# Two expert layers on one core: the out-projection spread over the products, a one-function gate in steps, wider slot tiles, and weights converted in place

## The chip, the cores and the metric

The kernel runs on one core of one Trainium2 chip. The metric is the device time of one execution in microseconds (us). Before the change the median of three runs is 2063.8 us (2063.78 to 2065.51). One further execution was profiled; everything called a row below comes from that one. Engines: PE is TensorE, DVE is VectorE, ACT is ScalarE, POOL is GpSimd, and SP is the queue that starts most transfers.

## What is computed

```python
def _attn_ref(x, state):                    # x (8,8,512,64), state (8,8,32,64)
    scores = x @ state^T / 8 ;  xread = softmax(scores) @ state
    scores2 = state @ x^T / 8 ; sread = softmax(scores2) @ x
    return concat([xread, sread], axis=2)   # 8 x 544 tokens of 512 numbers

def _moe_ref(x, expert_emb, tau, w1, w2):   # 8 experts, 512 -> 1024 -> 512
    idx, gate = the expert with the largest cosine to the token, its probability
    out[t] = gate[t] * (relu(x[t] @ w1[idx]) @ w2[idx])

def _moe2_ref(x, w_gate, w_val, w_out):     # dense, 512 -> 1536 -> 512
    g = x @ w_gate
    return (g * sigmoid(g) * (x @ w_val)) @ w_out
```

The three weights of the dense layer arrive as 64-bit floats. All products are float32 to nearly full precision: an operand is split into a high part H and a low part L, and one product is three matmuls (H by H, H by L, L by H; `mm3`, L136).

## The kernel before, in words

**Order of the work.** Python generators ("streams", L44 to L79) write the instructions of each engine in one fixed order. `main` is the stream that leads; at each of its yields every other stream gets one turn, and a stream that yields n sleeps for n turns. A yield of a function holds a stream back until the function is true; while `main` is held back, only the others put instructions into the queues. These waits exist only while the order is written. On the chip each engine runs its own queue strictly in that order and waits for semaphores, so an instruction that waits holds everything behind it on its engine.

**Stage 1, attention and the routed experts** (`attn_a`, `attn_b`, `route`, `groups` L593). The 8 batches of 512 tokens go mostly to one expert each. `groups` runs 8 batches of 8 pieces (n = 0 to 64); the result of a batch is scaled into the tile `xo` and stored to DRAM as `x2d[u]` (L642, L643).

**Stage 2, conversion** (stream `later`, `convert` L883). The dense weights are cut into 6 column pairs p. For each p six raw tiles (512 KB) are loaded (L901), narrowed from 64 to 32 bits (one ACT square L940, four DVE instructions L876 to L881), and combined by DVE into nine forms k = 0 to 8. `put` (L903) splits a form into the tile `cut` (ACT for H, POOL for L) and POOL starts its store to `w2d` (L907). The stream `homes` (L975) loads the forms of p = 0 to 2 back into their resident places, 2 transfers each (L973). `raw` and `cut` have two buffers each.

**Stage 3, the dense layer** (`moe2` L1035). There are 54 steps (u, p): eight units u of 512 tokens (R = 4 blocks of 128), and unit 8 of 256 tokens (R = 2), each by 6 pairs p. Only three pairs of weights are resident, so the order is units 0 to 6 by p = 0 to 2, unit 7 by p = 0 to 5 (weights replaced behind it: `refill`, L1149), units 0 to 5, then 8, then 6 by p = 3 to 5 (weights of p = 0 to 2 come back behind unit 6), and unit 8 by p = 0 to 2. A unit's first half is stored to `part` and added at its second half.

A step is seven Strassen-like products of 12 matmuls each (`prod`, L1106) into three PSUM banks, with adds between them that read a bank before the next product may go on accumulating in it:

```python
yield from prod(0, 0, True);  a = copy(bank 0)            # ACT,  L1128
yield from prod(1, 1, True);  u2 = bank 1 + a             # DVE,  L1130
yield from prod(0, 2);        Y[:, :, 0, 0] = copy(bank 0)  # ACT, L1132
yield from prod(1, 3);        u4 = bank 1 + a             # DVE,  L1134
yield from out(1)                        # 4 pieces for y1 of the step before
yield from prod(2, 4, True);  yield from prod(1, 5);  gate(1)
yield from out(0)                        # 4 pieces for y0 of the step before
yield from prod(2, 6);        gate(0)
```

`gate(j)` (L1119) is Sigmoid on ACT (L1121), two DVE products (L1122, L1123), and a split into `y{j}H` (ACT) and `y{j}L` (DVE). `out(j)` is the out-projection: R pieces of three matmuls 512 wide into `acc`. When a unit ends with "add", each piece loads its `old` from `part` first (L1056; one buffer) and DVE adds it (L1063). `x_forms` (L988) makes the seven operand forms xf0 to xf6 of the next unit from `x2r`, one after each product of the unit's last step; H is ACT's, L is DVE's.

**Beside it, unit 8's routed experts** (`slots` L759, `slots_scatter` L850), after the conversion: 8 slots, each 32 weight tiles of 128 x 256, loaded by SP (four buffers), split by ACT and DVE, two matmuls each; one PSUM buffer `ps` is shared by products and transposes. `main` can't fetch unit 8 before they are done (L1096).

Of the kernel before, what the change touches and what calls it, by code (L numbers as in the profile page):

```python
# [81 lines left out]
class W:  # L82
# [6 lines left out]
    obs = 2  # L89
    x_lo = ("dve",)  # L90
# [16 lines left out]
    s_gap = (4, 4)  # L107
# [3 lines left out]
    c_gap = (0, 2)  # L111
    c_lo = ("pool",)


class Kernel:
# [30 lines left out]
    def setup(self, cp, kp, dp):  # L146
# [12 lines left out]
        self.tauv = cp.tile([128, 32], F32, name="tauv")[:, 0:1]  # L159
        nc.sync.dma_start(self.tauv, self.tau.to_broadcast([128, 1]))  # L160
# [24 lines left out]

        cp.tile([128, 32], F32, name="fill_c")
# [139 lines left out]
    def attn_b(self, b):  # L326
# [132 lines left out]
    def spread_gate(self, g, R, u):  # L459
# [12 lines left out]
        pp, tag = (self.pa, "pa") if isinstance(u, int) else (self.pq, "pq")  # L472
# [120 lines left out]
    def groups(self):  # L593
# [12 lines left out]
        for n in range(65):  # L606
# [25 lines left out]
            for c in range(4):  # L632
                if prev is not None:
# [4 lines left out]
                    if pf == 7:  # L638
                        xo = self.hp.tile([128, 512], F32, tag="xo", name=f"xo{pb}_{c}", bufs=4)
# [119 lines left out]
    def slots(self):  # L759

        nc, lp = self.nc, self.lp
        regs = {}
        todo = [(e, i, k, c) for e in range(NCHK) for i, k, c in
                [(0, k, c) for k in range(4) for c in range(4)] + [(1, k, c) for c in range(2) for k in range(8)]]
        raw, w, at = {}, {}, [0, 0]

        def load():
# [8 lines left out]
            raw[n] = lp.tile([128, 256], F32, tag="raw", name=f"sraw{n}", bufs=4)  # L776
            nc.sync.dma_start(raw[n], src[ds(regs[e], 1), rows * 128:rows * 128 + 128, cols * 256:cols * 256 + 256]
# [3 lines left out]
        def split():  # L781
            n = at[1]
            if n == len(todo):
                return
            w[n] = [lp.tile([128, 256], F32R, tag="w" + k, name=f"sw{k}{n}", bufs=4) for k in "HL"]
            self.split(*w[n], raw.pop(n), lo_eng=W.s_lo[n % len(W.s_lo)])
            load()
            at[1] += 1

        for _ in range(4):  # L790
            load()
        for _ in range(3):
# [6 lines left out]
        n = 0  # L799
        x = load_x(0)  # L800
        for e in range(NCHK):
            hp = lp.tile([128, 8, 2, 64], F32R, tag="hp", name=f"shp{e}", bufs=1)
            yield W.s_gap[0]
            for k in range(4):
                ps = self.ps.tile([128, 512], F32, tag="ps", name=f"psl{e}_{k}")
                for c in range(4):
                    wH, wL = w.pop(n)
                    nc.tensor.matmul(ps[:, :256], x[:, c, :], wH, start=c == 0, stop=False)  # L808
                    nc.tensor.matmul(ps[:, :256], x[:, c, :], wL, start=False, stop=c == 3)
                    n += 1  # L810
                    split()
                    yield n % 2
                lo = lp.tile([64, 256], F32, tag="lo", name=f"slo{e}_{k}", bufs=1)
                nc.scalar.activation(lo, ps[64:128, :256], AF.Copy)
                hs = lp.tile([64, 256], F32, tag="hs", name=f"shs{e}_{k}", bufs=1)
                nc.vector.tensor_add(hs, ps[0:64, :256], lo)
                yield W.s_gap[1]
                pt = self.ps.tile([128, 512], F32, tag="ps", name=f"pst{e}_{k}")
                for i in range(2):
                    nc.tensor.transpose(pt[:, i * 64:(i + 1) * 64], hs[:, i * 128:(i + 1) * 128],  # L820
                                        self.ident[:64, :64])
                v = pt[:, 0:128].rearrange("p (i k) -> p i k", i=2)
                h = hp[:, 2 * k:2 * k + 2]
                nc.scalar.activation(h[:, :, 0, :], v, AF.Relu)
                nc.vector.scalar_tensor_tensor(h[:, :, 1, :], v, 0.0, h[:, :, 0, :].bitcast(F32),  # L825
                                               op0=ALU.max, op1=ALU.subtract)
            if e < NCHK - 1:
                x = load_x(e + 1)
            yield W.s_gap[1]
            for c in range(2):  # L830
                ps = self.ps.tile([128, 512], F32, tag="ps", name=f"sacc{e}_{c}")
                for k in range(8):
                    wH, wL = w.pop(n)
                    hl = hp[:, k].rearrange("p a k -> p (a k)")
                    nc.tensor.matmul(ps[:, :256], hl, wH, start=k == 0, stop=False)
# [549 lines left out]
```

## Time and profile before

| | |
|---|---|
| median of 3 runs | 2063.8 us |
| the profiled execution: its time, its span | 2068.23 us, 2066.8 us (1.4 us lie around the span) |
| busy share of the span | PE 75%, DVE 55%, ACT 33%, POOL 15% |
| granted clock of PE, mean | 0.862 |
| transfers | 227 MB, 29% of 16 DMA engines from SP's queue, 5% from POOL's |
| stage 1 alone | 0 to about 480 us |
| stage 1 with the conversion | 480 to 610 us |
| dense layer with the conversion | 610 to 850 us |
| dense layer with the slots | 850 to about 1640 us |
| dense layer alone | to 2067 us |

How to read the rows: in a timeline the columns are start, duration, engine, line, operation, output and inputs, count, and in brackets the idle time before and what ended it. Busy PE time overlaps itself (a matmul starts before the one in front has ended), so the pace of PE is read from the starts. A granted clock of 1 is 2.4 GHz, 0.5 is 1.2 GHz.

### The profile page before, as it was taken

The numbers are of one execution on the slowest core, as the hardware profiler recorded it, in microseconds if no ns is written. First come the engines' busy times: TensorE is split into PE (matmuls) and PEld (weight loads), VectorE is DVE, ScalarE is ACT, GpSimd is POOL, SyncE is SP. The second block draws the span as 40 slices with busy tenths as digits, with TensorE's granted clock in tenths as the row PEclk, the third lists the DMA queues.
The fourth block names the chain that finished last, engine by engine and source line by source line (L and its number), as shares of the span: only waits on it lengthen the run. The fifth ranks groups of instructions, "written<-read, shape, count | busy, mean of one in ns | idle before, by whom it ended". The sixth has DMA issues, their size and how long they took to land. (4 is left out here: it accounts for less than half of the span.)

```text
span 2066.8 us, 25792 instructions
## 1 busy us (share of the span) xinstructions
PE 1540.1 (75%) x8941; PEld 1361.6 (66%) x8942; DVE 1139.3 (55%) x2210; ACT 691.8 (33%) x1404; POOL 314.4 (15%) x316
## 2 busy tenths in 40 slices
PE   5799999997554444777878787888776866867876
PEld 4678787775443443676767677777766765756765
DVE  5677667785563665564555564555554533442432
ACT  4445455543322232333333333333332211211211
POOL 2343443332333323000000000000000000000000
PEclk8899999998676776898899999999977988987986
DMA  2243333244757544222223136622223121011441
GB/s 66 88 120 111 90 108 119 67 133 139 276 195 263 205 157 172 81 81 77 57 87 95 39 100 202 197 74 89 78 79 96 59 67 61 6 47 56 163 151 45
DMA packets 172619, 227.25 MB, mean 110 GB/s; under 512 B 49848, under 2 KB 114360, under 8 KB 170304
## 3 DMA queue, kind: packets, MB, share of 16 engines
q1 hardware_dynamic: 158992, 186.98, 28.8%
q0 software_dynamic: 13296, 38.28, 5.1%
q8 instruction: 72, 1.18, 0.2%
q14 instruction: 67, 0.55, 0.1%
q10 hardware_dynamic: 192, 0.26, 0.1%
HBM read 166.74 MB, written 68.16 MB: 114 GB/s over the span
## 5 line engine op out<-in xcount | busy, mean ns | idle before, releaser
L1112 PE MATMUL pq<-xf2H,hm 128*128 128x256 f32 (+1 forms) x432 | 125.9, 367 | 265.7 <-ACT u L1128 265.6
L1112 PEld LDWEIGHTS pq<-xf2H,hm 128*128 128x128 f32 x432 | 98.6, 262 | 275.1 <-ACT u L1128 275.1
L1121 ACT ACTIVATE sg<-Y 128x512 f32<-128x512 f32 (+1 forms) x108 | 65.5, 607 | 346.3 <-DVE Y L1139 177.4
L134 DVE TENSOR_TENSOR swL<-sraw,swH 128x256 fp32r<-128x256 f32 x256 | 104.1, 420 | 76.3 <-ACT swH L130 75.0
L141 PE MATMUL acc<-hH,w1H 128*128 128x512 f32 x256 | 111.6, 436 | 45.1 <-ACT w1H L130 34.0
L1112 PE MATMUL pq<-xf3H,hm 128*128 128x256 f32 (+1 forms) x432 | 119.7, 352 | 28.1 <-DVE u L1130 28.0
L1122 DVE TENSOR_TENSOR sg<-Y,sg 128x512 f32<-128x512 f32 (+1 forms) x108 | 75.0, 694 | 109.1 <-ACT sg L1121 109.1
L130 ACT ACTIVATE swH<-sraw 128x256 fp32r<-128x256 f32 x256 | 100.0, 409 | 84.6 <-PE psl L808 45.6
L1112 PEld LDWEIGHTS pq<-xf3H,hm 128*128 128x128 f32 x432 | 97.8, 259 | 32.5 <-DVE u L1130 32.4
L142 PE MATMUL acc<-hL,w1H 128*128 128x512 f32 x256 | 105.7, 413 | 8.5 <-DVE hL L622 8.5
L143 PE MATMUL acc<-hH,w1L 128*128 128x512 f32 x256 | 106.7, 417 | 3.9 <-POOL w1L L134 3.6
L1112 PE MATMUL pq<-xf1H,hm 128*128 128x256 f32 (+1 forms) x432 | 96.0, 299 | 5.0 <-DVE Y L1139 5.0
L1112 PE MATMUL pq<-xf5H,hm 128*128 128x256 f32 (+1 forms) x432 | 90.7, 288 | 5.7 <-DVE u L1134 5.7
L1112 PE MATMUL pq<-xf0H,hm 128*128 128x256 f32 (+1 forms) x432 | 93.5, 294 | 0.0
L1112 PE MATMUL pq<-xf6H,hm 128*128 128x256 f32 (+1 forms) x432 | 90.5, 289 | 3.9 <-DVE Y L1137 3.8
L141 PEld LDWEIGHTS acc<-hH,w1H 128*128 128x128 f32 x256 | 51.2, 200 | 58.0 <-ACT w1H L130 38.4
L1112 PE MATMUL pq<-xf4H,hm 128*128 128x256 f32 (+1 forms) x432 | 88.3, 284 | 0.0
L141 PE MATMUL o<-hm,y1H 128*128 128x512 f32 x204 | 86.1, 422 | 0.0
L808 PE MATMUL psl<-swH,sx 128*128 128x256 f32 x128 | 43.1, 337 | 57.5 <-DVE shp L825 50.0
L142 PE MATMUL o<-hm,y1H 128*128 128x512 f32 x204 | 84.4, 414 | 0.0
L141 PE MATMUL o<-hm,y0H 128*128 128x512 f32 x204 | 83.3, 408 | 1.0 <-ACT y0H L130 1.0
L143 PE MATMUL o<-hm,y1L 128*128 128x512 f32 x204 | 83.4, 409 | 0.0
(513 smaller groups left out, 4722.6 us busy)
## 6 DMA issues: line engine op xcount, KB each, us to landing
hm<-w2d SPq DMA_DIRECT2D x162, 256.0 KB
sraw<-in_moe_w SPq DMA_DIRECT2D x256, 128.0 KB
w2d<-cut POOLq DMA_DIRECT2D x54, 512.0 KB, 2.9
raw<-in_moe_w SPq DMA_DIRECT2D x32, 512.0 KB
raw<-in_moe_w SPq DMA_DIRECT2D x64, 256.0 KB
x2r<-x2d SPq DMA_DIRECT2D x15, 1024.0 KB
xr<-in_x SPq DMA_DIRECT2D x64, 128.0 KB
x2d<-xo SPq DMA_DIRECT2D x32, 256.0 KB
```

The costliest lines, as they stand in the source:

```text
L130: nc.scalar.activation(hi, src, AF.Copy)
L134: eng.tensor_sub(lo, src, hi.bitcast(F32))
L141: nc.tensor.matmul(ps, ah, bh, start=first and i == 0, stop=False)
L142: nc.tensor.matmul(ps, ah, bl, start=False, stop=False)
L143: nc.tensor.matmul(ps, al, bh, start=False, stop=last and i == n - 1)
L808: nc.tensor.matmul(ps[:, :256], x[:, c, :], wH, start=c == 0, stop=False)
L1112: nc.tensor.matmul(bank[b][:, g, :], l[:, cs], r[:, c, :], start=start and g == c == n == 0, stop=g == c == 1 and n == 2, skip_group_check ...
L1121: nc.scalar.activation(sg, Y[:, 0, j], AF.Sigmoid)
L1122: nc.vector.tensor_mul(sg, Y[:, 0, j], sg)
```

## The change

- **Order of a step.** The eight pieces of the out-projection (four of y1, then four of y0, of the step before) go between the products: two after product 1, one after 2, two after 3, one after 4, one after 5, the last after 6. The three banks get a name of their own each (`pq0` to `pq2`).
- **Gate.** `Silu` in place of `Sigmoid` and a DVE product; its instructions are issued in steps between products (the end of gate 0 in the next step). `y0L` is POOL's, `y1L` stays DVE's; `sg` has two buffers.
- **Operand forms.** All L parts of `x_forms` go to POOL; a21 is overwritten in place of a temporary.
- **Partial sums.** `old` is gone: `part` is loaded into `ob` itself (three buffers), two loads during y1's pieces, the others as buffers come free.
- **Conversion.** Pairs 0 to 2 are split straight into their resident places (no `cut`, no store, no load back), three raw buffers loaded ahead, two squares. The stream `keep` later stores these places to `w2d` from POOL's queue, for the refill. Pairs 3 to 5 are converted after the dense layer has begun, with larger gaps, three `cut` buffers and two raw buffers.
- **Order of units.** 7, 0 to 5, then 6 (all six pairs), 7, 0 to 4, 8, 5, 8. Unit 7's x2 stays on chip in `x2r`, into which stage 1 now writes all its `xo`; `main` builds its forms at the start of the dense layer (`prefetch` is gone). `main` starts a step when forms 0 to 6 of its pair exist, and asks for 7 and 8 at the step's end.
- **Slots.** 16 tiles of 128 x 512 a slot in place of 32 of 128 x 256, three buffers, other gaps; four transposes at a time.
- Small moves: `tauv` is loaded a few lines later; fill tiles go.

```diff
-    obs = 2
-    x_lo = ("dve",)
+    obs = 3
+    x_lo = ("pool",)
+    y_lo = ("gpsimd", "vector")
-    s_gap = (4, 4)
+    s_gap, s_step = (5, 4), 1
-    c_gap = (0, 2)
+    c_gap, c_gap2, c_lag, cuts, c_load = (0, 2, 1, 1), (2, 3, 2, 2), 2, 3, 3
+    h_lo = ("pool",)
+    k_gap = 6
...
-                        xo = self.hp.tile([128, 512], F32, tag="xo", name=f"xo{pb}_{c}", bufs=4)
+                        if c == 0:
+                            self.x2r = self.x2q.tile([128, 4, 512], F32, tag="x2r", name=f"xo{pb}")
+                        xo = self.x2r[:, c]
...
         def put(p, k, src):
-            t = cv.tile([128, 2, 512], F32R, tag="cut", name=f"cut{p}_{k}", bufs=2)
+            if p < NP // 2:
+                yield lambda: not self.routing and (2 * (NW * p + k) < 40 or self.w2b is not None)
+                w = self.W2.setdefault(p, {})
+                hm = [self.home(p, k, i) for i in range(2)]
+                h, l = hm if k > 6 else [t.rearrange("p (g c f) -> p g c f", g=2, c=2) for t in hm]
+                self.split(h, l, src, lo_eng=W.h_lo[k % len(W.h_lo)])
+                w[k] = hm
+                return
+            t = self.cut.tile([128, 2, 512], F32R, tag="cut", name=f"cut{p}_{k}", bufs=W.cuts)
...
+    def keep(self):
+        for p in range(NP // 2):
+            for k in range(NW):
+                for i in range(2):
+                    self.nc.gpsimd.dma_start(self.w2d[p, k, :, i, :].bitcast(F32), self.W2[p][k][i].bitcast(F32))
+                self.conv.add((p, k))
+                yield W.k_gap
...
+            def part():
+                r = len(obs)
+                if end is None or r == R:
+                    return
+                ob = gp.tile([128, 512], F32, tag="ob", name=f"ob{u}_{p}_{r}", bufs=W.obs)
+                if end == "add":
+                    nc.sync.dma_start(ob, self.part[u, :, r, :])
+                obs.append(ob)
+            for j in (1, 0):
+                for r in range(R):
+                    if j == 1 and r < W.obs - 1:
+                        part()
+                    self.mm3(acc[r], ...)
+                    if j == 0 and end is not None:
+                        if len(obs) == r:
+                            part()
+                        ob = obs[r]
+                        if end == "add":
+                            nc.vector.tensor_add(ob, acc[r], ob)
...
+                        part()
+                    yield
...
+                sg = gp.tile([128, 2, 256], F32, tag="sg", name=f"sg{j}{nm}", bufs=2)[:, :, :h]
+                nc.scalar.activation(sg, Y[:, 0, j], AF.Silu)
+                yield
                 nc.vector.tensor_mul(sg, Y[:, 1, j], sg)
+                yield
...
+                nc.scalar.activation(v[0], sg, AF.Copy)
+                yield
+                getattr(nc, W.y_lo[j]).tensor_sub(v[1], sg, v[0].bitcast(F32))
...
             yield from prod(1, 1, True)
             nc.vector.tensor_add(u2, bank[1], a)
+            if tail:
+                drain(tail)
+            turn()
+            yield from out(2)
...
             yield from prod(1, 5)
             nc.vector.tensor_add(Y[:, :, 1, 0], bank[1], a)
-            gate(1)
-            yield from out(0)
+            g1 = gate(1)
+            for _ in range(3):
+                next(g1)
+            turn()
+            yield from out(1)
             yield from prod(2, 6)
             nc.vector.tensor_add(Y[:, :, 0, 1], bank[2], u2)
-            gate(0)
+            drain(g1)
+            tail = gate(0)
+            for _ in range(2):
+                next(tail)
+            turn()
+            yield from out(8)
...
-            yield from self.convert(range(NP))
+            yield from self.convert(range(NP // 2), W.c_gap, 3, 2)
             close("cv")
+            yield lambda: self.gp is not None
+            st.add(self.keep())
...
+            yield from self.convert(range(NP // 2, NP), W.c_gap2, 2, 1)
```

## Rows read from the trace of the kernel before

**Rows 1.** Timeline of ACT: line L1132, once a step; steps 2, 6, 7, 31, 32.
```profile
670.60 0.58 ACT L1132 ACTIVATE Y<-pq 128x512 f32<-128x512 f32 x1
...
832.55 0.58 ACT L1132 ACTIVATE Y<-pq 128x512 f32<-128x512 f32 x1
857.70 0.60 ACT L1132 ACTIVATE Y<-pq 128x512 f32<-128x512 f32 x1 [0.77 <-PE pq L1112]
...
1478.15 0.60 ACT L1132 ACTIVATE Y<-pq 128x512 f32<-128x512 f32 x1
1513.57 0.60 ACT L1132 ACTIVATE Y<-pq 128x512 f32<-128x512 f32 x1 [2.90 <-PE pq L1112]
```

**Rows 2.** Timeline of PE at granted clock 1: first matmuls of three groups.
```profile
1682.25 0.28 PE L1112 MATMUL pq<-xf4H,hm 128*128 128x256 f32 x1
...
1685.13 0.39 PE L141 MATMUL o<-hm,y0H 128*128 128x512 f32 x1
...
1687.89 0.28 PE L1112 MATMUL pq<-xf6H,hm 128*128 128x256 f32 x1
```

**Rows 3.** Timeline of PE: products 0 and 2 of one R = 2 step.
```profile
1858.35 0.22 PE L1112 MATMUL pq<-xf0H,hm 128*128 128x128 f32 x1
...
1859.64 0.27 PE L1112 MATMUL pq<-xf1H,hm 128*128 128x128 f32 x1
...
1863.95 0.47 PE L1112 MATMUL pq<-xf2H,hm 128*128 128x128 f32 x1 [2.81 <-ACT u L1128]
...
1866.56 0.41 PE L1112 MATMUL pq<-xf3H,hm 128*128 128x128 f32 x1
```

**Rows 4.** Busy time by stage: stretch, length, PE, PEld, DVE, ACT, POOL, clock, DMA, GB/s.
```profile
480.00:610.00 130.00, 75.04 (x249) 54.32 (x248) 79.90 (x124) 41.01 (x73) 48.69 (x46) 0.74 0.59 207
610.00:850.00 240.00, 115.90 (x647) 105.98 (x645) 138.64 (x204) 68.31 (x118) 67.34 (x73) 0.71 0.53 191
850.00:1470.00 620.00, 492.11 (x3049) 447.45 (x3050) 338.49 (x641) 221.41 (x494) 16.80 (x31) 0.90 0.31 97
```

**Rows 5.** Waits, 610 to 850 us: us in total, times, longest.
```profile
PE pq L1112 <- ACT u L1128: 102.5, 6, 23.8
...
ACT cut L130 <- DMA w2d<-cut: 45.6, 16, 7.6
```

**Rows 6.** Waits of PE, 850 to 1470 us.
```profile
PE psl L808 <- DVE shp L825: 45.6, 21, 4.6
PE pq L1112 <- ACT u L1128: 42.1, 17, 6.3
```

**Rows 7.** Waits of PE, 1660 us to the end.
```profile
PE pq L1112 <- ACT u L1128: 99.2, 16, 15.5
```

**Rows 8.** Groups by line, whole span: busy us, mean ns, idle before and releasers.
```profile
L1123 DVE TENSOR_TENSOR sg<-Y,sg 128x512 f32<-128x512 f32 x96 | 66.4, 692 | 3.3
...
L1063 DVE TENSOR_TENSOR ob<-o,old 128x512 f32<-128x512 f32 x30 | 20.7, 690 | 84.9 <-DMA old<-part 74.3 <-issue 3.9 <-PE pq L1112 3.3
```

**Rows 9.** Groups by line of ACT and POOL, same columns.
```profile
L907 POOL DMA_DIRECT2D w2d<-cut x54 | 30.9, 572 | 17.1 <-POOL cut L134 14.3 <-issue 1.4 <-DMA w2d<-cut 1.2
L130 ACT ACTIVATE y1H<-sg 128x512 fp32r<-128x512 f32 x48 | 30.3, 631 | 73.5 <-DVE sg L1123 73.5
...
L134 POOL TENSOR_TENSOR cut<-q,cut 128x512 fp32r<-128x512 f32 x18 | 23.1, 1281 | 112.0 <-ACT cut L130 111.9
```

**Rows 10.** Timeline of ACT: the first conversion instruction.
```profile
486.38 0.65 ACT L940 ACTIVATE t(0, 'g', 0)_5620<-rawg 128x512 f32<-128x512 f32 x1
```

**Rows 11.** Timeline, 604 to 609 us: a POOL instruction, and DVE's conversion beside and behind it.
```profile
604.53 1.26 POOL L134 TENSOR_TENSOR w1L<-raw,w1H 128x512 fp32r<-128x512 f32 x1 [2.19 <-ACT w1H L130]
604.56 1.78 DVE L880 SCALAR_TENSOR_TENSOR t(2, 'g', 0)_6250<-t(2, 'g', 0)_6250,q 128x512 int32<-128x512 int32 x1
...
607.70 0.43 DVE L878 TENSOR_SCALAR q<-t(2, 'v', 0)_6276 128x512 int32<-128x512 int32 x1
608.64 0.68 DVE L880 SCALAR_TENSOR_TENSOR t(2, 'v', 0)_6276<-t(2, 'v', 0)_6276,q 128x512 int32<-128x512 int32 x1
```

**Rows 12.** Timeline of ACT: the last of two table loads, ahead of the first Sigmoid.
```profile
642.45 1.28 ACT L1121 ACT_TABLE_LOAD   x1
```

More of the change, by code (lines that the diff above doesn't have):

```diff
@@ new lines, in slots @@
+            ps = self.ps.tile([128, 512], F32, tag="ps", name=f"sacc{e}")
+            for k in range(8):
+                wH, wL = w.pop(n)
+                hl = hp[:, k].rearrange("p a k -> p (a k)")
+                nc.tensor.matmul(ps, hl, wH, start=k == 0, stop=False)
+                nc.tensor.matmul(ps, hl, wL, start=False, stop=k == 7)
+                n += 1
+                split()
+                yield W.s_step
+            lo = lq.tile([64, 512], F32, tag="lo", name=f"sro{e}", bufs=1)
@@ new lines, in forms @@
+            yield from put(p, 6, t)
+        for m in range(ahead):
+            load(m)
+            yield W.c_load
+        yield 4
+        for m, (p, nm, j) in enumerate(todo):
+            if self.wide and m not in sq:
+                square(m)
+                yield c_gap[2]
+            if nm == "g":
+                q[p, j] = cv.tile([128, 2, 4, 128], F32, tag=f"q{j}", name=f"q{p}_{j}", bufs=1)
+            if nm == "o":
+                dst = cv.tile([128, 512], F32, tag="t3", name=f"qo{p}_{j}", bufs=1)
+            else:
+                dst = q[p, j][:, "gv".index(nm)].rearrange("p c f -> p (c f)")
+            if self.wide:
+                yield from self.narrow(raw.pop(m), sq.pop(m), dst.bitcast(I32), c_gap)
+            else:
+                nc.vector.tensor_copy(dst, raw.pop(m))
+            load(m + ahead)
+            if nm == "o":
+                yield c_gap[3]
+                yield from put(p, 7 + j, dst)
+            elif nm == "v" and j == 1:
+                yield
+                yield from forms(p)
+            yield c_gap[1]
@@ L1075, in moe2, with out @@
+        prev = tail = None
+        def out(n):
+            if prev is not None:
+                for _ in range(n if prev_R == 4 else (n + 1) // 2):
+                    if next(prev, StopIteration) is not StopIteration:
+                        yield
         for i in range(len(steps) + 1):
             if i == len(steps):
-                for j in (1, 0):
-                    yield from out(j)
+                drain(tail)
+                yield from prev
                 return
@@ L1099, in moe2 @@
             nf = self.x_forms(self.x2r, nxt[1], f"{nxt[0]}_{nxt[2]}", self.x2p, xn) if nxt else None
[L1100 removed]
+            bank = [self.pq.tile([128, 512], F32, tag=f"pq{k}", name=f"pq{k}_{nm}") for k in range(3)]
             bank = [b.rearrange("p (g n) -> p g n", g=2)[:, :, :h] for b in bank]
@@ L1142, in moe2 @@
+            for _ in range(3):
+                next(g1)
+            turn()
+            yield from out(1)
             yield from prod(2, 6)
             nc.vector.tensor_add(Y[:, :, 0, 1], bank[2], u2)
-            gate(0)
-            prev = steps[i], y, w
+            drain(g1)
+            tail = gate(0)
+            for _ in range(2):
+                next(tail)
+            turn()
+            yield from out(8)
+            if weights is None:
+                yield lambda: 7 in w and 8 in w
```

288 lines of the change are left out of this document (122 added, 166 removed).

## The prediction

> **What bounds the kernel now.** I read first the timeline of ACT for L1132, which comes once a step, because its spacing shows the pace of the dense layer without any averaging. Steps 2 to 6 are 40.5 us apart ((832.55 - 670.60) / 4), steps 7 to 31 are 25.9 us apart ((1478.15 - 857.70) / 24), and step 32, which holds the "add" of a unit, takes 35.4 us [rows 1]. Next came the pace of PE where nothing holds it: 24 matmuls 256 wide in 2.88 us, 0.12 us each, and 12 matmuls 512 wide in 2.76 us, 0.23 us each [rows 2]. A full step is 84 of the one and 24 of the other: 10.1 + 5.5 = 15.6 us. In an R = 2 step twelve matmuls 128 wide take 1.29 us, so 84 take 9.0 us, and with 12 pieces' matmuls 11.8 us [rows 3]. So the reader sees three paces, 40.5, 25.9 and 35.4, against a floor of 15.6, to which the slots add 2.4 (below). PE's work is not what sets the end.
>
> Third, the stages: DVE is the busiest engine beside PE but has 42 to 45% left everywhere in the dense layer, and the clock granted to PE is 0.71 from 610 to 850 us and 0.90 later [rows 4]. Fourth, the waits name the cause. From 610 to 850 us PE stands 102.5 us before product 2, because ACT's copy of bank 0 (L1128) is late; and ACT is late because it stood 45.6 us before a `cut` buffer whose store had not landed, with that copy queued behind [rows 5]. With the slots, PE waits 45.6 us for the slots' DVE instruction after the transposes (21 times, 2.2 us) and 42.1 us for L1128 [rows 6]. After the slots the same L1128 is 99.2 us [rows 7]: gate 0 stands on ACT in front of it, and in the add steps DVE waits for `old`, 74.3 us in all [rows 8]. The slower clock comes with these idle stretches: the same product of 12 takes 1.29 us in one step and, behind a wait of 2.81 us, 2.61 us, which is the 1.2 GHz level [rows 3].
>
> **The change, part by part.**
>
> *Order of a step.* Pieces add no matmul, they only stand elsewhere. Between product 0 and product 2 there is now product 1 and two pieces, 1.44 + 1.38 = 2.8 us, where 1.44 was; between products 1 and 3, 3.5 us; between 3 and 5, and 4 and 6, 2.8 to 3.5 us. ACT's copy is as long as its other 512-wide ones, 0.63 [rows 9], and DVE's add 0.69 [rows 8]. y1 is asked for 5.7 us of PE work after product 5 and needs four ACT or DVE instructions and an add, 3.4 us; y0 is asked for 9 us after product 6 and needs about 4.5. So L1128's wait goes; what is late next is POOL's `y0L`, with everything on POOL queued before it.
>
> *Gate.* One DVE product of 0.69 goes twice a step; `y0L` moves from DVE's 0.69 to POOL's 1.28 [rows 8, 9]. DVE's own work falls from 11 to 8 instructions, 7.6 to 5.5 us. Silu has no row: I take Sigmoid's place in the queue at ACT's 0.63; the bound above is a table load of 1.28 us before each of 108 [rows 12], which ACT has room for, and below nothing.
>
> *Forms.* Seven L parts a unit, 0.69 each on DVE, become 1.28 each on POOL [rows 9]: 3.0 us of POOL a step, spread over three steps.
>
> *Partial sums.* The loads go two pieces to six pieces ahead. SP waits for the `ob` whose store is on its way before the fourth, with slot loads queued behind; product time up to its use is 4.3 us. DVE's 74.3 us [rows 8] go.
>
> *Stage 1's end and the first half of the conversion.* The conversion begins at 486 us [rows 10], and its loads now hold it 17 turns. Of stage 1 there remain 249 matmuls 512 wide [rows 4], 57 us, so its end is bounded by 543 and 609 us; I take 560, since 27 stores and 54 load-backs no longer hold ACT but DVE is nearly full. A raw tile costs DVE three times 0.68 and 0.43 [rows 11], 2.5 us; three pairs with forms cost 53 us, of which 13 pass beside stage 1. The remaining 40, two steps' own 11, forms 3 and locks 5 carry pair 2 to about 615 us; step 3 ends at **630**. `main` is held back in writing here, so PE idles. Bounds: 600 (DVE never held) and 690 (40 us steps).
>
> *Second half.* By the gaps a pair takes 88 turns, a step has 22, so three pairs take 12.2 steps. DVE a step: 5.5 + 0.9 (forms) + 4.4 (53 / 12.2) = 10.8 us. POOL: 1.3 + 3.0 + 4.1 (27 splits at 1.28 and issues at 0.57) + 2.5 (54 issues of `keep`, at 0.57 [rows 9]) = 10.9 us. Both fit in 15.6, but POOL's queue is filled in bursts: seven forms in 22 turns are 13 us of POOL beside 9 of the operand forms. Three `cut` buffers at 3 turns (2.1 us) cover 6.4 us of split and store. Bounds are 15.6 (all hidden) and 40.5 (as now); I take **21**, nearer the first, as half the stores, all first load-backs and the waits before product 2 are gone.
>
> *Slots.* 128 tiles of two matmuls at 0.23 are 59 us as 256 tiles at 0.12 were 61. By the gaps a slot is 69 turns, eight are 25.1 steps. PE a step: 15.6 + 2.4 + 0.2 = 18.2; DVE 5.5 + 0.9 + 3.5 + 1.3 = 11.2. Six turns now lie between the slots' DVE instruction and the product that waited 2.2 us for it [rows 6]. I take **18.9**; bounds 18.2 and 22. The scatter takes 2.7 more steps, so all is done 43 steps in; unit 8 is asked for before the 44th, and no wait is due.
>
> *Without cost:* bank names, `tauv`, the fill tiles and unit 7 first (its x2 is on chip, which saves one fetch) lie in queues that stand idle there; if that cover goes, each is one transfer. `refill` keeps its 108 loads behind units 6 and 5, SP waiting on PE as before, one unit earlier.
>
> **The sum.** 630; 12.2 x 21 = 256, to 886; 25.1 x 18.9 = 474, to 1360; up to step 45, 4.7 x 16.5 = 78; three full steps 49; six R = 2 steps at 13, 78; the tail (last gate 4, four pieces 3, adds, store and its landing) 14: a span of 1579. With the 1.4 us around it, 1580, against 2068.2 for the profiled execution. That one lies 0.2% above the median, so 1578 is the forecast. About 0.2% is also what a measurement here can tell from no change.
>
> **Rivals.** *The conversion still holds ACT* (1816 us): the 12.2 steps stay at 40.5. For it: 45.6 us of waits for stores [rows 5], on the same ACT queue. Against: fewer stores a step, a third buffer. It decides if a store's cycle passes 6.4 us.
>
> *POOL locks DVE* (1767 us). A DVE instruction with two on-chip-memory inputs that began with a POOL split took 1.78 us, not 0.68 [rows 11]. The change adds 54 `y0L` and 119 form splits on POOL; if each stops DVE for 1.09 us and PE waits for all of it, that is 189 us on top. Against: DVE has 4 us spare a step, and bank adds have one input in PSUM. The Trainium skill, SBUF — State Buffer, section Who interferes with whom, says that such DVE and POOL instructions exclude each other for a whole instruction, which speaks against moving splits to POOL. By that rule the time is at worst this rival's; the row agrees with it.
>
> *The clock stays low* (slower, 2165 us). Pieces and products alternate over three banks, and each handover can leave a short gap; if PE never gets back to 2.4 GHz for long, its 879 us of work (48 x 15.6, 6 x 11.8, 59) stretch by the clock. At 0.71, as from 610 to 850 us [rows 4], that adds 359 us (1937); below 0.645 it passes the kernel before, and at 0.6 it adds 586. For it: both clock levels in neighbouring products [rows 3]. Against: from 850 to 1470 us a clock of 0.90 with PE idle for 21% (620 - 492 us) [rows 4].
>
> **Chances.** The forecast, from 1480 to 1730: 0.80; conversion 0.06; lock in full 0.07; clock 0.04; better than 1480 (stage 1 ending at 545, conversion hidden at 16) 0.03. The ends come from the bounds: 630 down to 600, 21 to 17 and 18.9 to 18.2 give 1482; up, 690, 25 and 20.5 give 1729. Faster by over 0.2% holds all but the clock rival and a hundredth: 0.95; same 0.01, slower 0.04.
>
> **What would show it.** L1132's spacing at 16 to 17 us without and 18 to 20 with slots, 18 to 25 in the second conversion; no wait of PE for the copy of bank 0 above some 10 us in all; no DVE wait for `part`; the first product at 555 to 580 us; a clock above 0.95 after 900 us. Wrong if ACT waits for `cut` stores by tens of us, if pieces wait for `y0L`, or if `main` waits at unit 8 with PE idle.

## The result, and the profile after

The changed kernel takes 1548.15 us (median of four runs, 1544.77 to 1548.78) against 2064.66 us for the kernel before in the same runs: a ratio of 0.749, 95% interval 0.748 to 0.751. Predicted were 1578 us, with a range of 1480 to 1730. The profiled execution took 1547.96 us with a span of 1546.4. Of the four executions of `u1_order` below one took 7597 us and the other three 1618.0 to 1623.0 us; its median, 1621.7 us, is that of all four (1620.4 without the long one).

| | before | after |
|---|---|---|
| PE busy | 75% | 91% |
| DVE, ACT, POOL busy | 55%, 33%, 15% | 67%, 43%, 36% |
| granted clock, mean | 0.862 | 0.956 |
| transfers | 227 MB | 212 MB |

**The pace.** The line that copies bank 0 after product 2, L1132 before, is L1190 after, and is the same clock of steps. Its timeline (start, duration, engine, line, operation, and the idle time before it), for steps 1, 3, 4, 16, 41, 42, 43, 48 and 49:

```profile
554.53 0.60 ACT L1190 ACTIVATE Y<-pq 128x512 f32<-128x512 f32 x1 [2.51 <-PE pq L1155]
...
621.99 0.60 ACT L1190 ACTIVATE Y<-pq 128x512 f32<-128x512 f32 x1 [2.68 <-PE pq L1155]
642.96 0.60 ACT L1190 ACTIVATE Y<-pq 128x512 f32<-128x512 f32 x1 [3.21 <-PE pq L1155]
...
861.26 0.60 ACT L1190 ACTIVATE Y<-pq 128x512 f32<-128x512 f32 x1 [3.20 <-PE pq L1155]
...
1332.57 0.60 ACT L1190 ACTIVATE Y<-pq 128x512 f32<-128x512 f32 x1 [3.46 <-PE pq L1155]
1348.61 0.60 ACT L1190 ACTIVATE Y<-pq 128x512 f32<-128x512 f32 x1 [2.15 <-PE pq L1155]
1364.22 0.60 ACT L1190 ACTIVATE Y<-pq 128x512 f32<-128x512 f32 x1 [2.73 <-PE pq L1155]
...
1441.59 0.38 ACT L1190 ACTIVATE Y<-pq 128x256 f32<-128x256 f32 x1 [1.30 <-PE pq L1155]
1454.08 0.60 ACT L1190 ACTIVATE Y<-pq 128x512 f32<-128x512 f32 x1 [2.03 <-PE pq L1155]
```

The second conversion (steps 4 to 16) goes at 218.3 / 12 = 18.2 us a step, the stretch with the slots (16 to 41) at 471.3 / 25 = 18.9, an undisturbed step takes 15.6, a step of half width 12.5. Before, a step took 40.5 us beside the conversion, 25.9 beside the slots and 35.4 with an "add" [rows 1]; no step after the fourth now takes more than 25 us.

The stages after, in the columns of [rows 4]:

```profile
480.00:640.00 160.00, 117.12 (x561) 98.84 (x562) 124.04 (x167) 63.51 (x113) 77.47 (x54) 0.79 0.32 102
640.00:870.00 230.00, 209.13 (x1366) 188.23 (x1364) 179.27 (x206) 88.36 (x155) 137.65 (x150) 0.96 0.56 200
870.00:1310.00 440.00, 433.53 (x2823) 391.90 (x2824) 291.39 (x403) 204.49 (x363) 113.87 (x92) 0.99 0.48 155
1310.00:1540.00 230.00, 225.13 (x1602) 209.08 (x1600) 104.69 (x171) 66.06 (x131) 55.63 (x54) 1.00 0.42 139
```

The one weak stretch is the first, 480 to 640 us: PE idles for 43 us of 160 and the clock is 0.79. From 640 us on PE is busy for 868 of 900 us and the granted clock is 0.96 to 1.00, where it was 0.71 and 0.90.

Waits of PE (us in total, times, longest), first 480 to 640 us, then 640 to 870 us:

```profile
PE pq L1155 <- ACT hm L133: 20.0, 4, 9.1
PE pq L1155 <- POOL hm L137: 5.7, 4, 2.1
...
PE pq L1155 <- DVE Y L1198: 6.7, 3, 5.1
PE pq L1155 <- DVE u L1184: 5.0, 5, 3.1
...
PE pq L1155 <- ACT u L1179: 0.4, 1, 0.4
```

The copy of bank 0 (L1179, the old L1128) cost 102.5 us from 610 to 850 us [rows 5]; it costs 0.4 here, 0.7 beside the slots and nothing later (42.1 and 99.2 in [rows 6, 7]). What PE waits for in the first stretch are weight forms of pairs 1 and 2. The chain of waits that ended last there (start, length, what) shows how they come about:

```profile
606.53 0.70 DVE q L888
607.26 0.70 DVE tA L936
607.99 0.64 ACT hm L133
...
609.92 5.38 POOL hm L137 x4
615.35 2.52 PE pq L1155 x10
```

DVE narrows the last tile that forms 0 to 6 of pair 2 need, and then POOL makes four L parts one behind the other, 5.4 us, before PE goes on with step 3. From 618.6 to 632.6 us the chain is mostly DVE's again: it narrows the two tiles of forms 7 and 8, which are asked for only at the step's end, with adds of step 3 queued behind them (see `u5_dve`).

### The profile page after: what moved, and what is told of

It is laid out like the page before. It is cut to its first block, busy times and chain, and to the rows that moved or that the text cites. A ratio compares the mean times of both kernels' runs of the same rounds, so it can differ in the third digit from the quotient of the medians.

```text
span 1546.4 us, 23969 instructions
## 1 busy us (share of the span) xinstructions
PE 1410.5 (91%) x8685; PEld 1243.1 (80%) x8686; DVE 1032.6 (67%) x1753; ACT 657.7 (43%) x1228; POOL 558.0 (36%) x500
## 4 chain that ended last, share of the span: by engine, by line
PE 47%; DVE 11%; issue 4%; ACT 3%; POOL 2%; DMA 2%; SPq 0%; POOLq 0%; ACTq 0%; DVEq 0%
PE pq L1155 28%; PE o L144 5%; PE o L146 5%; PE o L145 5%; DVE sg L1169 1%; ACT sg L1167 1%; PE psl L813 1%; PE psl L812 1%; PE sacc L841 1%; POOL hm L137 1%; DVE swL L137 1%; PE sacc L840 1%; DVE q L885 1%; DMA sraw<-in_moe_w 1%; DMA w2d<-cut 1%
## 5 line engine op out<-in xcount | busy, mean ns | idle before, releaser
L137 DVE TENSOR_TENSOR swL<-sraw,swH 128x512 fp32r<-128x512 f32 x128 | 113.5, 902 | 67.6 <-ACT swH L133 61.6
L1175 POOL TENSOR_TENSOR y0L<-sg,y0H 128x512 fp32r<-128x512 f32 (+1 forms) x54 | 74.6, 1382 | 216.0 <-ACT y0H L1173 196.2
L133 ACT ACTIVATE swH<-sraw 128x512 fp32r<-128x512 f32 x128 | 77.5, 623 | 70.2 <-DMA sraw<-in_moe_w 28.2
L137 POOL TENSOR_TENSOR w1L<-raw,w1H 128x512 fp32r<-128x512 f32 x32 | 46.3, 1446 | 167.2 <-ACT w1H L133 167.2
L1155 PE MATMUL pq<-xf0H,hm 128*128 128x256 f32 (+1 forms) x432 | 90.9, 291 | 14.2 <-ACT hm L133 12.7
L1155 PE MATMUL pq<-xf3H,hm 128*128 128x256 f32 (+1 forms) x432 | 89.0, 287 | 7.4 <-DVE u L1184 7.4
L1155 PE MATMUL pq<-xf2H,hm 128*128 128x256 f32 (+1 forms) x432 | 89.2, 287 | 2.3 <-ACT u L1179 2.3
L1155 PEld LDWEIGHTS pq<-xf0H,hm 128*128 128x128 f32 x432 | 73.9, 198 | 18.2 <-ACT hm L133 13.3
L1194 DVE TENSOR_TENSOR u<-pq,u 128x512 f32<-128x512 f32 (+1 forms) x54 | 35.6, 659 | 76.2 <-PE pq L1155 75.8
L1155 PEld LDWEIGHTS pq<-xf6H,hm 128*128 128x128 f32 x432 | 73.2, 196 | 16.1 <-DVE Y L1198 14.0
L1155 PEld LDWEIGHTS pq<-xf1H,hm 128*128 128x128 f32 x432 | 73.6, 197 | 15.6 <-ACT hm L133 7.9
```

Of the source, the lines that this page charges most:

```text
L133: nc.scalar.activation(hi, src, AF.Copy)
L137: eng.tensor_sub(lo, src, hi.bitcast(F32))
L1155: nc.tensor.matmul(bank[b][:, g, :], l[:, cs], r[:, c, :], start=start and g == c == n == 0, stop=g == c == 1 and n == 2, skip_group_check ...
L1175: getattr(nc, W.y_lo[j]).tensor_sub(v[1], sg, v[0].bitcast(F32))
L1194: nc.vector.tensor_add(u4, bank[1], a)
```

## The experiments

All times are medians of four or five runs; the interval is that of the ratio to the kernel before (2064 to 2068 us in every group of runs). Each run edits the changed kernel, except `b1_moe2`, which edits the kernel before.

| run | what | us | against 1548 | ratio, 95% |
|---|---|---|---|---|
| `u1_order` | old order of pieces | 1621.7 | +74 | 0.782 to 0.788 |
| `u2_gate` | gates in one go | 1594.8 | +47 | 0.770 to 0.775 |
| `u7_sig` | Sigmoid and a DVE product | 1594.0 | +46 | 0.770 to 0.774 |
| `u3_order_gate` | the first two | 1698.9 | +151 | 0.820 to 0.826 |
| `u37_step` | all three | 1784.5 | +236 | 0.861 to 0.866 |
| `u4_old` | old partial sums | 1632.8 | +85 | 0.787 to 0.795 |
| `u6_conv` | conversion packed, two `cut` | 1606.2 | +58 | 0.774 to 0.782 |
| `u8_slots` | old slots | 1647.5 | +99 | 0.793 to 0.801 |
| `u5_dve` | L parts back to DVE | 1536.9 | -11 | 0.740 to 0.747 |
| `v1_conv1` | first conversion denser | 1561.8 | +14 | 0.755 to 0.759 |
| `v2_both` | the last two | 1538.2 | -10 | 0.743 to 0.746 |
| `b1_moe2` | before, with the new step | 1713.7 | +166 | 0.827 to 0.832 |

The pace of each, worked out from the same line's timeline as above (us a step):

| run | steps 4 to 16 | 16 to 41 | 41 to 54 | step 42 to 43 |
|---|---|---|---|---|
| changed kernel | 18.2 | 18.9 | 14.8 | 15.6 |
| `u1_order` | 19.6 | 20.3 | 16.4 | 15.8 |
| `u2_gate` | 19.5 | 19.7 | 15.2 | 16.5 |
| `u7_sig` | 19.7 | 19.7 | 14.9 | 15.6 |
| `u3_order_gate` | 21.2 | 21.7 | 17.8 | 16.8 |
| `u37_step` | 23.0 | 23.3 | 19.2 | 18.8 |
| `u4_old` | 18.3 | 20.0 | 18.0 | 15.6 |
| `u5_dve` | 17.5 | 18.9 | 14.8 | 15.6 |

### The step: order, gate, function

`u1_order`, the old places of the pieces, four after product 3 and the rest after product 5:

```diff
             yield from prod(1, 1, True)
...
-            yield from out(2)
             yield from prod(0, 2)
...
-            yield from out(1)
             yield from prod(1, 3)
...
-            yield from out(2)
+            yield from out(4)
             yield from prod(2, 4, True)
...
-            yield from out(1)
             yield from prod(1, 5)
...
-            yield from out(1)
+            yield from out(8)
             yield from prod(2, 6)
```

> The changed kernel with one part undone: the pieces of the out-projection stand as before, four after product 3 and four after product 5; the gate stays in steps. Theory (cover): ACT's copy of bank 0 stands behind Silu of gate 0 alone; from the end of product 6 it needs 0.69 + 0.63 + 0.63 and handoffs, some 2.3 us, and products 0 and 1 give 2.9 us, so no wait before product 2 returns: 1548 to 1565 us. Rival (the order carries the gain): a wait of 1.4 to 2 us before product 2 in each of 54 steps returns, 1620 to 1660 us.

Measured: 1621.7 us, the rival's figure, but not by the wait that the rival named. The wait for the copy of bank 0 comes back only in part: 11.0, 14.0 and 7.4 us in the three stretches from 640 us on, 32 us in all, 0.6 us a step. The wait for DVE's add before product 3 (L1184) is 19.0, 8.6 and 1.7 us, where the changed kernel has 5.0 in all. Another part, which overlaps these, is in the add steps: step 32 takes 1194.80 - 1169.69 = 25.1 us where the changed kernel's takes 18.8, and steps 35, 38, 41 and 44 take 24.0 to 27.0. The add's group of DVE (busy, mean ns, idle before it and what ended that), in this run and in the changed kernel:

```profile
L1096 DVE TENSOR_TENSOR ob<-o,ob 128x512 f32<-128x512 f32 x30 | 20.2, 688 | 31.3 <-DMA ob<-part 28.7 <-PE o L146 1.9 <-PE sacc L841 0.6
```

```profile
L1096 DVE TENSOR_TENSOR ob<-o,ob 128x512 f32<-128x512 f32 x30 | 20.7, 689 | 10.8 <-PE o L146 10.4 <-DMA ob<-part 0.2
```

The loads stand at the same pieces as in the changed kernel; with four pieces in a row, those that must wait for an `ob` to come free have no product left to hide behind. So the order works twice: it gives the copies and adds their time, and it gives the loads theirs.

`u2_gate`, both gates issued whole where the old step had them, in the new order:

```diff
-            for _ in range(3):
-                next(g1)
+            drain(g1)
...
-            tail = gate(0)
-            for _ in range(2):
-                next(tail)
...
+            drain(gate(0))
```

> The changed kernel with one part undone: each gate is issued whole (gate 1 after product 5, gate 0 at the step's end), ahead of the next step's copy of bank 0; the new order of the pieces and Silu stay. Theory (cover): the copy is ready some 3.6 us after product 6 (add 0.69, Silu 0.63, product 0.69, split 0.63, copy 0.63 and handoffs), and one piece, products 0 and 1 and two pieces give 4.9 us, so PE does not wait: 1548 to 1570 us. Rival (the steps of the gate carry the gain): 1 to 1.5 us a step return, 1600 to 1630 us.

Measured: 1594.8 us. Below the rival's range and far above the theory's. PE waits for the copy of bank 0 for 17.1, 6.1 and 3.8 us: gate 0's last ACT copy, which needs DVE's product, stands in front of it again. Nearly all of the loss lies where another stream works beside the step; from step 41 on it is 0.4 us a step.

`u3_order_gate`, both edits together:

> The changed kernel with both undone: old order of the pieces, and each gate issued whole; Silu stays. Theory (cover): the copy of bank 0 is ready 3.6 us after product 6 and is asked for after 2.9 us, 0.8 us of wait before product 2 in each of 54 steps, 40 to 50 us, if the clock stays: 1585 to 1610 us, more than the two parts alone add up to. Rival (one of the two carries it): as much as that part alone.

`u37_step`, and the old function too, with the DVE product that it needs:

```diff
-                nc.scalar.activation(sg, Y[:, 0, j], AF.Silu)
+                nc.scalar.activation(sg, Y[:, 0, j], AF.Sigmoid)
                 yield
+                nc.vector.tensor_mul(sg, Y[:, 0, j], sg)
```

> The changed kernel with the whole step undone: old order of the pieces, each gate whole, and Sigmoid with a DVE product in place of Silu. Theory (cover): 0.69 us more on the way to the copy of bank 0, so 1.5 us of wait a step, 75 to 100 us: 1620 to 1660 us, with the wait for the copy of bank 0 near 80 us in the waits of PE. Rival (what the kernel before lost came from the conversion and the partial sums, not from the step): under 1590 us.

Measured: 1698.9 and 1784.5 us, both above what I expected. The wait for the copy of bank 0 from 640 to 870 us, first with order and gate undone, then with the function too:

```profile
PE pq L1154 <- ACT u L1178: 37.3, 11, 8.2
```

```profile
PE pq L1154 <- ACT u L1179: 50.5, 10, 10.4
```

Over all three stretches it is 32, 27, 93 and 150 us for order, gate, both, and all three. Order and gate together cost 30 us more than the sum of each alone: either one leaves the copy most of its time, and only with both gone does it stand behind a whole gate with 1.44 us of product to hide in. It is the same wait as in the kernel before, brought back by three edits. The time lost is more than the waits: with all three undone the granted clock is 0.87, 0.93 and 0.90 in the three stretches, where the changed kernel has 0.96, 0.99 and 0.98, and DVE waits 30.4 us for `part` again.

`u7_sig`, the function alone, with order and gate as in the changed kernel:

> The changed kernel with Sigmoid and one more DVE product in place of Silu, and nothing else: 108 more DVE instructions of about 0.69 us, 74 us of DVE work. Theory (with the gate in steps DVE has several us spare a step, so the extra product is covered): 1548 to 1560 us, PE waits for y1L and y0L below 15 us in all. Rival (each stands in the chain from product 5 to the pieces of y1 and PE waits for it): 108 times 0.5 to 0.8 us, 1600 to 1635 us. With the old order and the whole gate the same product had cost 86 us.

Measured: 1594.0 us, so the theory is wrong and the rival's range is a little too high. The timeline of this run, steps 4, 16, 41, 42 and 43:

```profile
643.77 0.60 ACT L1191 ACTIVATE Y<-pq 128x512 f32<-128x512 f32 x1 [2.34 <-PE pq L1155]
...
879.57 0.60 ACT L1191 ACTIVATE Y<-pq 128x512 f32<-128x512 f32 x1 [2.09 <-PE pq L1155]
...
1372.09 0.60 ACT L1191 ACTIVATE Y<-pq 128x512 f32<-128x512 f32 x1 [3.97 <-PE pq L1155]
1388.13 0.60 ACT L1191 ACTIVATE Y<-pq 128x512 f32<-128x512 f32 x1 [0.91 <-PE pq L1155]
1403.75 0.60 ACT L1191 ACTIVATE Y<-pq 128x512 f32<-128x512 f32 x1 [0.29 <-PE pq L1155]
```

Step 43 takes the same 15.6 us, so the product is hidden there, though ACT comes to the copy 0.29 us before bank 0 is ready and no longer 2.73. Beside the conversion the step goes from 18.2 to 19.7, beside the slots from 18.9 to 19.7. Two products of 0.69 us cost 1.5 and 0.8 us there, although DVE is idle for a fifth of the conversion stretch in this run (186.97 us busy of 230). PE's waits show where: from 640 to 870 us `y1H` is late by 9.8 us in all (1.8 in the changed kernel) and the add before product 3 by 10.3 (5.0). Spare time on DVE covers the product only where it lies at the right place in the queue.

### Partial sums

`u4_old`: the add takes its old value from a tile of one buffer, loaded just ahead of its piece, and `ob` has two buffers; order and gate stay new.

```diff
-                if end == "add":
-                    nc.sync.dma_start(ob, self.part[u, :, r, :])
...
+                    if j == 0 and end == "add":
+                        old = gp.tile([128, 512], F32, tag="old", name=f"old{u}_{p}_{r}", bufs=1)
+                        nc.sync.dma_start(old, self.part[u, :, r, :])
...
-                            nc.vector.tensor_add(ob, acc[r], ob)
+                            nc.vector.tensor_add(ob, acc[r], old)
```

> The changed kernel with one part undone: a partial sum is loaded into a tile of its own with one buffer, one load a piece of y0 (and two output buffers). Theory (the order hides it): the load of the next piece starts when the add before has read the tile, some 3.5 us before its own add, and a product and a piece give 2.1 us, so DVE waits about 1.4 us three times in each of 8 units; PE's spare time takes most of it: 1550 to 1580 us. Rival (the early loads carry the 74 us that the kernel before lost): 1605 to 1625 us.

Measured: 1632.8 us, above the rival's range. DVE's wait, 870 us to the end, is that of the kernel before (74.3 us in [rows 8]):

```profile
DVE ob L1097 <- DMA old<-part: 67.2, 24, 5.0
```

Add steps take 25.5 to 27.9 us among the slots. So the new order alone does not hide these loads, as the early loads alone did not in `u1_order` (28.7 us of DVE's waits): both are needed. A slower clock takes part of the 85 us: from 1310 to 1620 us the granted clock is 0.85 in this run, where the changed kernel has 1.00 from 1310 to 1540.

### Conversion

`u6_conv`: the second conversion with the first one's gaps, and two `cut` buffers (two edits in one; the run doesn't part them).

```diff
-    c_gap, c_gap2, c_lag, cuts, c_load = (0, 2, 1, 1), (2, 3, 2, 2), 2, 3, 3
+    c_gap, c_gap2, c_lag, cuts, c_load = (0, 2, 1, 1), (0, 2, 1, 1), 2, 2, 3
```

> The changed kernel with the second conversion bunched: the gaps of the first conversion, and two buffers for the stored forms. Theory (spreading matters): ACT stands before the stores again with the copies of the banks queued behind, steps of 25 to 35 us over some 7 steps, then nothing: 1570 to 1630 us. Rival (the sum of DVE's and POOL's work decides, not its spread): 1540 to 1560 us.

Measured: 1606.2 us, as the theory said, though the shape is another. Timeline of steps 5 to 8, and ACT's wait from 640 to 870 us:

```profile
660.06 0.59 ACT L1190 ACTIVATE Y<-pq 128x512 f32<-128x512 f32 x1
697.66 0.58 ACT L1190 ACTIVATE Y<-pq 128x512 f32<-128x512 f32 x1
718.73 0.58 ACT L1190 ACTIVATE Y<-pq 128x512 f32<-128x512 f32 x1
755.26 0.60 ACT L1190 ACTIVATE Y<-pq 128x512 f32<-128x512 f32 x1 [0.76 <-PE pq L1155]
```

```profile
ACT cut L133 <- DMA w2d<-cut: 33.5, 12, 5.6
```

Steps 6, 8 and 10 take 37 to 38 us, nearly the 40.5 of [rows 1], with steps of 19 to 21 us between them, and not some seven of 25 to 35. They are the steps with a pair's seven forms (eight splits into `cut` in step 6, seven in step 8, one or two in 7 and 9). The rival "the conversion still holds ACT" is thus true of a packed conversion. PE waits there for the copy of bank 0 (16.6 us), for DVE's adds L1184 and L1194 (13.7 and 12.9) and for `y1H` (10.0). Gaps and third buffer together keep ACT from standing there (it waits 7.8 us for these stores in the changed kernel).

`v1_conv1`: the first conversion written in fewer turns.

```diff
-    c_gap, c_gap2, c_lag, cuts, c_load = (0, 2, 1, 1), (2, 3, 2, 2), 2, 3, 3
+    c_gap, c_gap2, c_lag, cuts, c_load = (0, 1, 0, 0), (2, 3, 2, 2), 2, 3, 1
```

> The changed kernel with the first conversion written in fewer turns: gaps of 0, 1, 0, 0 turns in place of 0, 2, 1, 1, and its loads one turn apart in place of three. Theory (steps 1 to 3 are held because pair 2's forms are written late): step 3 ends some 20 to 35 us earlier and everything behind it moves with it, 1515 to 1535 us. Rival (DVE is the limit from 480 to 620 us, so conversion placed earlier pushes stage 1's own instructions back by as much): 1543 to 1565 us.

Measured: 1561.8 us, the rival. Timeline of steps 1, 3 and 4:

```profile
573.25 0.58 ACT L1190 ACTIVATE Y<-pq 128x512 f32<-128x512 f32 x1
...
621.88 0.57 ACT L1190 ACTIVATE Y<-pq 128x512 f32<-128x512 f32 x1
638.48 0.60 ACT L1190 ACTIVATE Y<-pq 128x512 f32<-128x512 f32 x1 [2.69 <-PE pq L1155]
```

Step 1 comes 19 us later, step 3 at the same 622 us and step 4 only 4.5 us sooner: the conversion pushes stage 1 back by nearly what it gains. Steps 4 to 16 then take 231 us, not 218, with 8.6 us of PE's waits going to POOL's `y0L`, a wait that the changed kernel doesn't have. Why the later stretch suffers isn't settled; the same work of POOL meets the steps at another phase.

### The slots

`u8_slots`: the slots as in the kernel before, which is 256-wide tiles, four buffers, two transposes at a time and the old gaps; the run doesn't part these.

> The changed kernel with the slots as before: 32 tiles of 256 a slot, four buffers, the old gaps. Theory: the products wait again for the DVE instruction after the transposes (32 times, some 2 us), the slots take 640 turns in place of 552, so they end 4 steps later and the leading stream is held before unit 8 for some 25 to 35 us: 1610 to 1650 us. Rival (the spare time of the step hides the narrow tiles too): 1548 to 1575 us.

Measured: 1647.5 us, as the theory said. Timeline of steps 43 and 44, and PE's wait from 870 to 1420 us:

```profile
1427.51 0.60 ACT L1187 ACTIVATE Y<-pq 128x512 f32<-128x512 f32 x1 [2.36 <-PE pq L1152]
1485.96 0.60 ACT L1187 ACTIVATE Y<-pq 128x512 f32<-128x512 f32 x1 [3.41 <-PE pq L1152]
```

```profile
PE psl L812 <- DVE shp L829: 25.8, 22, 3.1
```

The old slots take more turns, so unit 8 is not ready: step 44 lasts 58.5 us where the changed kernel's lasts 20.1. The other 63 us by step 43 are in the slots' steps themselves, the wait for the DVE instruction after the transposes among them (45.6 us in [rows 6]).

### L parts on POOL or on DVE

`u5_dve`:

```diff
-    x_lo = ("pool",)
-    y_lo = ("gpsimd", "vector")
+    x_lo = ("dve",)
+    y_lo = ("vector", "vector")
```

> The changed kernel with one part undone: the L parts of the operand forms and of y0 are DVE's again, not POOL's. Theory (PE is the bound from 870 us on, the lock is hidden): DVE has 2.3 us more a step and loses the time that POOL held it; nothing behind 870 us, some us in the second conversion, where DVE is busy for 42 of 50 us: 1540 to 1570 us. Rival (POOL's instructions hold DVE, and PE waits for it): faster, 1500 to 1540 us. Rival (DVE's spare time is what the change lives on): 1590 us and more.

Measured: 1536.9 us; its interval (0.740 to 0.747) lies below that of the changed kernel (0.748 to 0.751). The slots' L part on DVE (busy, mean ns), in the changed kernel and in this run:

```profile
L137 DVE TENSOR_TENSOR swL<-sraw,swH 128x512 fp32r<-128x512 f32 x128 | 113.5, 902 | 67.6 <-ACT swH L133 61.6 <-PE o L145 3.5 <-PE sacc L841 1.7
```

```profile
L137 DVE TENSOR_TENSOR swL<-sraw,swH 128x512 fp32r<-128x512 f32 x128 | 85.8, 687 | 59.8 <-ACT swH L133 59.5
```

The same instruction, not touched by the edit, is 215 ns shorter in the mean without these splits on POOL. The gain in time lies before step 16 alone: step 4 comes 5 us sooner and steps 4 to 16 take 8 us less. In step 3 the timelines show how; first the changed kernel, then this run:

```profile
620.22 1.77 DVE L883 SCALAR_TENSOR_TENSOR t(2, 'o', 0)_6639<-t(2, 'o', 0)_6639,rawo 128x512 f32<-128x512 f32 x1
622.02 1.41 DVE L885 TENSOR_SCALAR qo<-t(2, 'o', 0)_6639 128x512 int32<-128x512 int32 x1
...
632.50 0.68 DVE L1198 TENSOR_TENSOR Y<-pq,u 128x512 f32<-128x512 f32 x1
```

```profile
620.50 0.68 DVE L883 SCALAR_TENSOR_TENSOR t(2, 'o', 0)_6639<-t(2, 'o', 0)_6639,rawo 128x512 f32<-128x512 f32 x1
...
628.79 0.68 DVE L1198 TENSOR_TENSOR Y<-pq,u 128x512 f32<-128x512 f32 x1
```

Three of the four DVE instructions that narrow each of the last two tiles of pair 2 take 1.14 to 1.77 us beside POOL's L parts, where they take 0.43 to 0.69 in this run, L885 with its one input among them. So the add that product 6 of step 3 waits for (L1198) begins 3.7 us sooner in this run. Beside the slots, where some 28 us of DVE were lost, PE hardly waited for DVE (3.3 us of 440 in the changed kernel), and the pace is the same 18.9.

`v2_both` joins this to `v1_conv1`:

> The shorter first conversion of the run beside it, and the L parts of the operand forms and of y0 back on DVE, which alone gave 1536.9 us. Theory (the two act in different stretches, so they add): the time of the shorter conversion alone less 9 to 13 us, 1505 to 1528 us. Rival (both draw on the same spare time of DVE between 550 and 640 us): no better than the better one of the two alone, 1530 to 1550 us.

Measured: 1538.2 us, 23.6 us better than `v1_conv1` alone and no better than `u5_dve` alone: the rival. With the L parts on DVE the denser conversion costs nothing and brings nothing. `u5_dve` is the best version seen, 0.7% under the changed kernel.

### The new step in the kernel before

`b1_moe2`: order, gate, Silu, forms and partial sums of the changed kernel; conversion, order of units and slots of the kernel before.

> The kernel before with the new step alone: pieces between the products, gate in steps with Silu, operand forms and y0L on POOL, partial sums loaded into ob, three named banks. Conversion with stores and load-backs, order of units and 256-wide slots stay as before. Theory (the step is the larger part of the gain, and the waits for the copy of bank 0 go even beside the old conversion): steps with slots 19 to 21 us in place of 25.9, add steps below 22, the first steps, beside the conversion, still 30 to 38 us because ACT waits for stores; 1680 to 1800 us. Rival (conversion and slots carry more than half of the 516 us): above 1810 us. The two undo runs so far (step in whole +236, spreading +58, slots +99) leave some 120 us to the weights kept in place and to what the parts do together.

Measured: 1713.7 us, as the theory said: 351 of the 516 us are the step's. Timeline of steps 7 and 8, and ACT's wait from 640 to 860 us:

```profile
834.44 0.60 ACT L1169 ACTIVATE Y<-pq 128x512 f32<-128x512 f32 x1 [1.14 <-PE pq L1134]
857.41 0.60 ACT L1169 ACTIVATE Y<-pq 128x512 f32<-128x512 f32 x1 [0.85 <-PE pq L1134]
```

```profile
ACT cut L131 <- DMA w2d<-cut: 30.6, 14, 4.5
```

The new step is worth little beside the old conversion: step 7 comes at 834 us, 23 us ahead of [rows 1], because ACT still waits for stores; PE's wait for the copy of bank 0 is still 23.3 us from 640 to 860 us, where the theory had it gone. The step is worth nearly all of its 351 us behind the conversion. The changed kernel passes step 8 at 714.4 us, 143 us ahead of this run, and that is most of the 166 us that conversion, order of units and slots add. Unit 8 doesn't wait in this run (step 44 takes 15.6 us) although the slots are the old ones: they begin at 808 us, beside step 6, and in `u8_slots` at 872 us, beside step 16. So the long step 44 of `u8_slots` belongs to old slots behind a late conversion. No run takes back the weights kept in place, the order of units or the names of the banks alone, and what each brings is not shown.

## Why the prediction was right, point by point

The time was 30 us under the forecast and inside its range; the verdict and the mechanism hold. Step by step, against the sum (630, 256, 474, 219):

- **Stage 1 and step 3.** Predicted 630 for the end of step 3. Step 4's line at 643.0, less product 0 to 2 and two pieces (5.7 us), gives 637. The parts were off both ways: the first product comes at 541.2 us (predicted 555 to 580), 2 us under the lower bound of 543, and steps 1 to 3 take longer. "`main` is held back in writing here, so PE idles" was not the reason: written earlier, step 3's line came no sooner and step 4's 4.5 us sooner (`v1_conv1`). DVE's narrowing and the four POOL splits behind each other are in the chain; moving those splits was not tried.
- **Second half of the conversion.** This is the term that was mis-sized: 12.2 steps at 18.2 us, not 21, which is 34 us and more than the whole error. Three buffers and the gaps left ACT 7.8 us of waits for stores, so 21 was too near the old pace. POOL's load a step was as worked out (137.65 / 230 x 18.2 = 10.9 us); DVE's was 14.2, not 10.8. The longer instructions beside POOL are in it: from 640 to 870 us 206 instructions keep DVE busy for 179 us, where `u5_dve` has 256 in 173. So the step got by with less spare time on DVE than the sum gave it.
- **Slots.** Predicted 18.9, measured 18.9. PE's own 18.2 was worked out and the 0.7 above it taken, so that it is met to the tenth is luck. Unit 8 doesn't wait (step 44: 20.1 us). `u8_slots` shows both halves of that step: without it the pace is about 21 and unit 8 waits.
- **The rest.** Predicted 219 us from there to the end, measured 1546.4 - 637 - 222 - 473 = 214. The floor of 15.6 is met to the tenth, a half step is 12.5 for 13.
- **"So L1128's wait goes".** It went, but not by the order alone, as that step argued: taking back the order returns 32 us of it, the gate 27, both 93, and the DVE product makes it 150. The argument left out that the gate's place counts nearly as much.
- **"What is late next is POOL's `y0L`".** Wrong for the changed kernel, where PE waits for DVE's adds and for weight forms; only `v1_conv1` shows it.
- **Gate.** Silu brought one table load of 1.28 us, not 108, so the value taken held. But the DVE product was counted as DVE load only. It is worth 46 us, all where conversion and slots stand beside the step.
- **Partial sums.** DVE's wait for `part` fell from 74.3 to 0.2 us, as predicted. The cover named, product time, is there only with the new order (`u1_order`) and the early loads (`u4_old`) together.
- **Rivals.** The lock of DVE by POOL is real, but taking the added POOL splits back returns 11 us, not 189. That is the lock less the work that DVE then does itself; the lock alone has no run. The rival let PE wait for every stretched instruction, and most were off PE's path. The Trainium skill, SBUF — State Buffer, section Who interferes with whom, says that the two exclude each other; the row of 902 against 687 ns agrees with it. The clock did not stay low: it is 0.79 in the stretch where PE idles for 43 of 160 us and 0.99 beside the slots.

## What to carry to other kernels

When two engines hand results to a third in a fixed order, put independent work of the third between each pair, and issue a chain of several engines one link at a time; here taking back both cost 151 us, and each alone 74 and 47. An engine's spare share is no cover by itself: an instruction that is free in a lone step cost its full time beside the conversion. A conversion or any other side stream is best spread to the pace of what runs beside it: the same work, packed and with one buffer less, brought 37 us steps back.

## What the runs showed of the hardware that was not expected

The prediction priced the lock on DVE's side alone. The timeline of the changed kernel, 603 to 618 us (POOL and DVE), shows it on both:

```profile
603.41 1.35 POOL L137 TENSOR_TENSOR hm<-q,hm 128x512 fp32r<-128x512 f32 x1 [11.56 <-ACT hm L133]
603.56 1.75 DVE L883 SCALAR_TENSOR_TENSOR t(2, 'v', 1)_6562<-t(2, 'v', 1)_6562,rawv 128x512 f32<-128x512 f32 x1
...
611.14 1.71 POOL L137 TENSOR_TENSOR hm<-tB,hm 128x512 fp32r<-128x512 f32 x1
...
616.66 0.69 DVE L1026 TENSOR_TENSOR xs<-xs,x2r 128x512 f32<-128x512 f32 x1
616.76 1.74 POOL L137 TENSOR_TENSOR hm<-tA,hm 128x512 fp32r<-128x512 f32 x1 [1.47 <-ACT hm L133]
...
617.96 0.69 DVE L1184 TENSOR_TENSOR u<-pq,u 128x512 f32<-128x512 f32 x1 [0.61 <-PE pq L1155]
```

In the pair at 603 us and in the pair at 616 us the one that begins second is the longer: DVE takes 1.75 us where it begins 0.15 us behind POOL, and POOL takes 1.74 us, not its 1.26 to 1.35, where it begins 0.10 us behind DVE. The split at 611.14, one of the four in the chain of the first stretch, takes 1.71 us; a DVE instruction of 1.73 us, begun at 609.99, ran when it began. So DVE's work lengthens POOL's part of that chain too. The add of a bank (L1184), with one input in PSUM, begins while that POOL instruction still runs and takes its usual 0.69 us. The Trainium skill, SBUF — State Buffer, section Who interferes with whom, says that the order of issue decides who blocks; these two pairs agree with it.

Silu costs 0.606 us in the mean over its 108 uses, like the Sigmoid that it replaces, and stands among copies and squares without a switch: the trace has one table load at its first use and none later.
